# Parking half of the attention results in DRAM, three conversion buffers in the first pass over the weights, and other planner settings

## The chip, the cores and the metric

The kernel runs on one core of a Trainium2 chip. A core has a matrix engine (TensorE, PE in the profile), a vector engine (VectorE, DVE), a scalar engine (ScalarE, ACT), GpSimd (POOL, which here only issues DMAs) and a sync engine (SyncE, SP, which only issues DMAs). They run side by side, each through its own queue in a fixed order, and wait for one another by semaphores. The metric is the device time of one execution in microseconds (us).

## The reference

An attention over 4 batches and 12 heads (448 tokens, 64 columns a head) is followed by one MoE-like block. In short:

```
scores = cap * tanh(q @ k.T / sqrt(64) / cap)
attn   = softmax(scores) @ v                    # per batch and head
x      = heads side by side                     # (4, 448, 768)
u      = x + (x.T @ U @ V).T                    # mixing over the tokens, rank 32
out    = u + max(u @ w_ch1, 0) @ w_ch2          # 768 -> 3072 -> 768
```

`U`, `V`, `w_ch1` and `w_ch2` arrive as 64-bit floats and are read as pairs of 32-bit words. Every product of the block is made of three fp32r matmuls (high by high, high by low, low by high).

## The kernel before, in words

**Attention.** Heads are handled in pairs of 128 rows; a step takes two pairs, so there are 12 steps (three per batch). A step loads q, k and v, makes the scores on PE into PSUM (L417), tanh on ACT with a per-partition scale held in `qsc` (L422), exp on ACT (L430), the products with v on PE (L443, L455), sums of the exponentials on DVE (L462) and a last sum over partitions on PE (L491). The sums go through DMAs from POOL (L496, L501, L514: spread over partitions, to DRAM, back as a broadcast) and scale the result on DVE (L518). Two steps later the mixing follows (`mixin`: transposes L540, high and low parts, products L555 and L576, addition L580). The result of batch b stays in the SBUF tile `u<b>` (128 x 6 x 448).

**Conversion.** The weights are 48 blocks of 128 x 768. Each is loaded as 64-bit words into `wr` (L631, 768 KB), turned into fp32 by four operations (`convert`: an absolute value on ACT L299, a shift L306 on DVE or L304 on ACT, a sign L311 and a join L315 on DVE) and written to DRAM as `kept` (L635). Later it is read back as `wa` (L644). There is one `wr` and one `wc` for most blocks; the first eight may also use a second pair.

**MoE.** Two passes, batches 0 and 1, then 2 and 3; each has 12 chunks of two blocks of w_ch1 and two of w_ch2. In a chunk the up product is done by seven Strassen products of 9 matmuls (L728), whose weight sums `ws` (L601, L608) are made on DVE and ACT from `wa`; the results go through `cx` (L741) and relu (L254, L710) into `g`. The down product has 12 groups of 6 matmuls (L791); three groups stay in PSUM over all chunks (`acc`), the other nine are added to `u` on DVE (L796). A chunk is 135 matmuls. The operands `x` of a pass are made from `u` (L601, L608).

**The order.** A planner in the kernel (`Plan.simulate`) walks through all tasks with a duration for each, a latency for each DMA, a priority and a first time (`begin`), gives every engine its list of instructions, and `emit` writes them out in that order. The numbers in it only set the order: on the chip each engine waits at the head of its own list. Pools (`Pool`) hold SBUF and PSUM room; a pool with `after` opens when the pools named there are closed, and closing waits for everything in them.

**Names that the change touches:** the pools `up` (the four `u` tiles, for the whole kernel), `cv` (one `wr`, one `wc`), `ax` (small attention tiles) and `le`; the constants `ALONE`, `EARLY`, `START`, `PACE`, `NEAR`; the tasks in `convert`, `two`, `normalize`, `mixin`, `converted`, `moe` and `down`.

Of the kernel before, what the change touches and what calls it, by code (L numbers as in the profile page):

```python
# [11 lines left out]
F32 = mybir.dt.float32  # L12
# [3 lines left out]
AF = mybir.ActivationFunctionType  # L16
ALU = mybir.AluOpType
# [15 lines left out]

ALONE = 22

EARLY = 14

# [3 lines left out]

FLOOR = 1

FIRST = 8

START, PACE = 9000, 7000

NEAR = 2

# [223 lines left out]
class Build(Plan):  # L273
    def __init__(self, tc, qk, v, u, vv, w1, w2, cap, ident, out):
        super().__init__()
        self.tc, self.nc = tc, tc.nc
        self.qk, self.v, self.u, self.vv = qk, v, u, vv
        self.w, self.cap, self.id_dram, self.out = (w1, w2), cap, ident, out
        PSUM = bass.MemoryType.PSUM
        self.cp = Pool("cp", {"const": 1})  # L280
        self.up = Pool("up", {"u%d" % b: 1 for b in range(B)})
        self.cv = Pool("cv", {"wr": 1, "wc": 1})
        self.pre = Pool("pre", {"th": 4, "qk": 1, "es": 2, "wr": 1, "wc": 1})
        self.ax = Pool("ax", {"sr": 1, "r7": 2, "rb": 2, "xh": 1, "xl": 1, "ys": 1}, side="right")
        self.ap = Pool("ap", {"qk": 3, "vn": 2, "th": 3, "es": 2}, side="right")
        self.xp = Pool("xp", {"x": 7, "cx": 4, "ta": 2, "wa": 2, "ws": 2}, after=(self.pre,))
        self.lt = Pool("lt", {"ws": 5, "w1": 2, "g": 5}, after=(self.ap,))
        self.le = Pool("le", {"w1": 1, "g": 2}, after=(self.ax,), side="right")
        self.px = Pool("px", {"sc": 1, "o": 1}, space=PSUM, side="right")
        self.ps = Pool("ps", {"sc": 1, "o": 1, "misc": 2}, space=PSUM)  # L290
        self.pm = Pool("pm", {"mm": 3}, after=(self.px,), space=PSUM, side="right")
        self.pl = Pool("pl", {"mm": 5 - len(STAY), "acc": len(STAY)}, after=(self.ps,), space=PSUM)
        self.dp = None

    def convert(self, raw, raw_t, a, a_t, prio, n):
# [5 lines left out]
        def low(e):  # L301
            half = raw_t().bitcast(U16)
            if e is nc.scalar:
                e.activation(out=half[:, 0::4], in_=half[:, 1::4], func=AF.Copy, scale=2.0 ** -13, bias=2.0 ** -14 - 0.5)  # L304
            else:
                e.tensor_scalar(  # L306
                    out=half[:, 0::4], in0=half[:, 1::4], scalar1=13, scalar2=None, op0=ALU.logical_shift_right)
# [11 lines left out]
        self.task({"ACT": 190 + 0.8 * n}, absolute, r=[(raw, "u")], w=[(a, 0)], prio=prio)  # L319
        self.task({"DVE": 1.08 * n, "ACT": 190 + 0.8 * n} if FLOOR else {"DVE": 1.08 * n}, low, r=[(raw, "l")], w=[(raw, "l0")], prio=prio)  # L320
        self.task({"DVE": 1.08 * n}, sign, r=[(raw, "u"), (raw, "l0")], w=[(raw, "l1")], prio=prio)
# [17 lines left out]
    def mixing_consts(self):  # L339
        nc = self.nc  # L340
        begin, prio = 4000, -150
        raw = self.buf("wr", [128, 2 * DM], I32, self.cv, self.pre)
# [23 lines left out]

        self.task({"SP": 700}, load, w=[(raw, "u"), (raw, "l"), ("ident", 0)], lat=4000, begin=begin, prio=prio)
        self.task({"SP": 1400}, load2, w=[(raw2, "u"), (raw2, "l")], lat=4500, begin=begin, prio=prio)
        self.convert(raw, lambda: raw.t[:TM, :2 * n], a, lambda: a.t[:TM, :n], prio, n)
# [4 lines left out]
    def attention(self):  # L374
        self.u_bufs = [self.buf("u%d" % b, [128, NP, S], F32, self.up) for b in range(B)]
        for p in range(0, B * NP + 2 * LAG, 2):
            if p < B * NP:
                self.two(p)
                self.normalize(p + 1)
            if p >= 2 * LAG:  # L380
                self.mixin((p - 2 * LAG) // NP, (p - 2 * LAG) % NP // 2)
# [8 lines left out]
    def two(self, p):  # L390
# [5 lines left out]
        for i, qk in enumerate(qks):  # L396

            def load(i=i, qk=qk):
                nc.sync.dma_start(out=qk.t, in_=self.qk[b, p % NP + i])

            self.task({"SP": 350}, load, w=[(qk, 0)], lat=4000, prio=prio)
        self.task({"SP": 350}, lambda: nc.sync.dma_start(out=vn.t, in_=self.v[b, p % NP // 2]), w=[(vn, 0)], lat=4500, prio=prio)
        REST = (0, 1), 3
        groups = [((0, 0), (0, 1)), ((0, 2), REST), ((1, 0), (1, 1)), ((1, 2),)]
        where = {}
        for steps in groups:
            th = self.buf("th", [128, 2, 2, S], F32, *pools)
            for j, (i, t) in enumerate(steps):
# [12 lines left out]
                def tanh(j=j, ps=ps, th=th):  # L421
                    nc.scalar.activation(out=th.t[:, j], in_=ps.t[:, :, :S], func=AF.Tanh, scale=self.qsc)  # L422

# [55 lines left out]
    def normalize(self, p):  # L479
# [24 lines left out]
        self.task({"DVE": 540, "ACT": 440}, lambda e: self.copy(e, sr.t, s.t[:, :S]), r=[(s, 0)], w=[(sr, 0)], prio=prio)  # L504
        self.task({"POOL": 4000}, spread, r=[(sr, 0)], w=[(r7, 0)], lat=2000, prio=prio)
        self.task({"DVE": 150}, lambda: nc.vector.reciprocal(r7.t, r7.t), w=[(r7, 0)], prio=prio)
        self.task({"POOL": 1000}, put, r=[(r7, 0)], w=[("rd", p)], lat=2500, prio=prio)
        for i, q in enumerate((p - 1, p)):
# [10 lines left out]

            self.task({"POOL": 2000}, get, r=[("rd", p)], w=[(rb, 0)], lat=2900, prio=prio)  # L520
            self.task({"DVE": 538}, norm, r=[(rb, 0)], w=[(u, q % NP)], prio=prio)

    def mixin(self, b, pp):
# [48 lines left out]
        for i in range(2):  # L572
# [9 lines left out]
            self.task({"PE": 210}, mix, r=[(ys, 0), ("vst", 0)], w=[(hh, 0)], prio=prio, mode="mm")  # L582
            self.task({"DVE": 538}, add, r=[(hh, 0)], w=[ks[i]], prio=prio)

    def operands(self, bs, prio):
# [13 lines left out]
    def parts(self, ps, sums, ts, made, terms, n, prio, tag, d, halves):  # L599
# [17 lines left out]
        for p in ps:  # L617
# [3 lines left out]
                w=[(ts[p], 2 * d + 1)], prio=prio)  # L621

    def converted(self, which, f, prio):
        nc = self.nc
        pools = (self.cv, self.pre) if len(self.raws) < FIRST else (self.cv,)
        raw = self.buf("wr", [128, 2 * DM], I32, *pools)
# [9 lines left out]

        self.task({"SP": 350}, load, w=[(raw, "u"), (raw, "l")], lat=4800, prio=prio, begin=START + PACE * (len(self.raws) - 1))
        self.convert(raw, lambda: raw.t, a, lambda: a.t, prio, DM)
        self.task({"ACT": 120}, keep, r=[(a, 0)], w=[("kept", which, f)], lat=5000, prio=prio)

    def block(self, which, f, prio):
        nc = self.nc
        a = self.buf("wa", [128, DM], F32, self.xp)
        self.task({"SP": 350}, lambda: nc.sync.dma_start(out=a.t, in_=self.kept[which, f]),  # L644
            r=[("kept", which, f)], w=[(a, 0)], lat=3500, prio=prio)
        return a
# [29 lines left out]
    def moe(self):  # L676
# [6 lines left out]
        for n, bs in enumerate(((0, 1), (2, 3))):  # L683
            xs = self.operands(bs, -50)
            for c in range(NCH):
                fs = [c * CF + i for i in range(CF)]
                ws = self.strassen_weights(c, 3)
                w1 = {f: self.weights(f, 3) for f in fs}
                gs = {}
# [12 lines left out]
        for _ in self.down(order, *pend):  # L702
            pass

    def relu(self, b, f, src, key, gs):
# [68 lines left out]
    def down(self, order, bs, fs, w1, g, c):  # L774
        nc = self.nc
        last = c == NCH - 1
        for i, b in enumerate(bs):
            u = self.u_bufs[b]
            for d in range(ND):
# [15 lines left out]
                def add(ps=ps, d=d, u=u):  # L795
# [3 lines left out]
                    w=[(ps, 0)], prio=at, mode="mm")  # L799
                if last or not stay:  # L800
                    self.task({"DVE": 538}, add, r=[(ps, 0)], w=[(u, d)], prio=-200)
# [62 lines left out]
```

## Time and profile before

| | |
|---|---|
| median of the timed runs | 939.3 us |
| the profiled execution | 933.91 us, of it the span 932.1 us |
| PE busy | 875.0 us, 94% of the span |
| DVE busy | 710.7 us, 76% |
| ACT busy | 443.7 us, 48% |
| DMA | 123.47 MB, 132 GB/s over the span |
| mean granted clock of PE | 0.987 of full speed |

Busy times are averages over stages with different limits, so the stages have to be read apart: attention until about 228 us (its last sum over partitions), the rest of its normalization and mixing until about 262 us with the first MoE chunk beside it, the first pass until about 598 us, and the second pass until 928 us.

### The profile page before, as it was taken

To read this page: it belongs to the slowest core of one execution; us is meant where nothing else is said; L and a number is where in the kernel's file an instruction comes from. 1 tells how busy PE (TensorE), PEld (TensorE's weight loads), DVE (VectorE), ACT (ScalarE), POOL (GpSimd) and SP (SyncE) were. 2 spreads that over 40 slices of the span, in tenths; PEclk is the share of its full clock that TensorE was granted. 3 is DMA by queue.
4 is the path that set the end of the run, shared out by engine and by line. 5 is a ranking of instruction groups with operands and counts; after the bars stand their busy time and mean duration, and the time that the engine had idled before them with its cause. 6 is when DMAs were issued, how large, how long until landed. Compare 5 with 4: busy or idle time off the path is not lost. (4 is left out here: it accounts for less than half of the span.)

```text
span 932.1 us, 11540 instructions
## 1 busy us (share of the span) xinstructions
PE 875.0 (94%) x4320; PEld 686.9 (74%) x4320; DVE 710.7 (76%) x1153; ACT 443.7 (48%) x623; POOL 59.3 (6%) x112
## 2 busy tenths in 40 slices
PE   6879999889598999999999999899999999999998
PEld 2223333335497898888888898799999999999997
DVE  4778989998778788797887979976556666655654
ACT  6988899987434333343334433432222233322320
POOL 0222322232100000000000000000000000000000
PEclk9999999999799999999999999999999999999999
DMA  7675565324644555645555442431121222112113
GB/s 246 223 240 198 168 214 173 107 64 148 200 156 150 169 189 162 210 140 182 187 165 208 139 153 82 150 87 50 36 69 51 69 68 69 36 49 69 51 52 119
DMA packets 41176, 123.47 MB, mean 132 GB/s; under 512 B 6960, under 2 KB 11040, under 8 KB 41120
## 3 DMA queue, kind: packets, MB, share of 16 engines
q1 hardware_dynamic: 29984, 98.17, 33.8%
q10 hardware_dynamic: 6912, 18.88, 5.1%
q0 software_dynamic: 4224, 5.68, 2.1%
q8 instruction: 34, 0.56, 0.2%
q14 instruction: 22, 0.18, 0.1%
HBM read 98.16 MB, written 24.47 MB: 132 GB/s over the span
## 5 line engine op out<-in xcount | busy, mean ns | idle before, releaser
L728 PE MATMUL mm<-x,ws 128*128 128x448 f32 x1512 | 334.7, 369 | 10.3 <-DVE ws L608 5.4
L728 PEld LDWEIGHTS mm<-x,ws 128*128 128x128 f32 x1512 | 284.1, 189 | 40.2 <-DVE cx L741 7.9
L791 PE MATMUL mm<-g,w 128*128 128x448 f32 x1296 | 288.7, 367 | 7.2 <-DVE cx L741 6.7
L791 PEld LDWEIGHTS mm<-g,w 128*128 128x128 f32 x1296 | 242.2, 188 | 31.2 <-DVE cx L741 9.3
L796 DVE TENSOR_TENSOR u<-u,mm 128x448 f32<-128x448 f32 x216 | 132.5, 621 | 85.2 <-PE mm L791 84.3
L791 PE MATMUL acc<-g,w 128*128 128x448 f32 x432 | 99.2, 365 | 0.0
L254 ACT ACTIVATE g<-cx 128x448 fp32r<-128x448 f32 x72 | 41.7, 580 | 119.1 <-DVE cx L741 118.9
L417 PE MATMUL sc<-qk 64*128 64x448 f32 (+1 forms) x384 | 82.9, 596 | 15.7 <-ACT th L422 10.7
L422 ACT ACTIVATE th<-sc,qsc 128x896 f32<-128x896 f32 x84 | 82.2, 1022 | 8.7 <-PE sc L417 6.7
L791 PEld LDWEIGHTS acc<-g,w 128*128 128x128 f32 x432 | 81.0, 188 | 6.8
L254 ACT ACTIVATE cx<-mm 128x448 f32<-128x448 f32 x72 | 39.1, 543 | 97.7 <-PE mm L728 97.5
L254 ACT ACTIVATE ws<-ta 128x384 fp32r<-128x384 f32 x83 | 43.5, 524 | 76.3 <-DVE ta L601 73.3
L430 ACT ACTIVATE th<-th,capt 128x1792 f32<-128x1792 f32 (+1 forms) x48 | 77.5, 1620 | 0.6 <-ACT th L422 0.3
L299 ACT ACTIVATE wc<-wr 128x768 f32<-128x768 f32 (+2 forms) x50 | 45.3, 906 | 60.5 <-DMA kept<-wc 44.6
L417 PEld LDWEIGHTS sc<-qk 64*128 64x128 f32 (+1 forms) x384 | 26.8, 178 | 57.5 <-ACT th L422 32.7
L306 DVE TENSOR_SCALAR wr<-wr 128x768 uint16<-128x768 uint16 (+2 forms) x39 | 40.0, 1026 | 35.9 <-DMA wr<-in_w 27.1
L741 DVE TENSOR_TENSOR cx<-cx,mm 128x448 f32<-128x448 f32 x72 | 44.8, 623 | 28.3 <-PE mm L728 28.0
L455 PE MATMUL o<-th,vn 128*64 128x448 f32 x276 | 58.2, 556 | 0.5 <-ACT th L430 0.4
L608 DVE TENSOR_TENSOR ws<-ta,ws 128x384 fp32r<-128x384 f32 x96 | 53.6, 560 | 4.8 <-ACT ws L254 3.9
L311 DVE TENSOR_SCALAR wr<-wr 128x768 uint16<-128x768 uint16 (+2 forms) x50 | 50.9, 1018 | 5.7 <-ACT wr L304 5.5
L462 DVE TENSOR_TENSOR es<-es,th 128x896 f32<-128x896 f32 (+1 forms) x48 | 51.9, 1080 | 3.8 <-ACT th L430 3.2
L315 DVE SCALAR_TENSOR_TENSOR wc<-wc,wr 128x768 int32<-128x768 int32 (+2 forms) x50 | 47.0, 940 | 2.6 <-ACT wc L299 1.3
(70 smaller groups left out, 692.9 us busy)
## 6 DMA issues: line engine op xcount, KB each, us to landing
wr<-in_w SPq DMA_DIRECT2D x48, 768.0 KB, 5.6
wa<-kept SPq DMA_DIRECT2D x96, 384.0 KB, 3.1
kept<-wc ACTq DMA_DIRECT2D x48, 384.0 KB, 5.8
qk<-in_qk SPq DMA_DIRECT2D x24, 448.0 KB, 4.3
vn<-in_v SPq DMA_DIRECT2D x12, 448.0 KB, 4.4
rb<-rd POOLq DMA_DIRECT2D x48, 112.0 KB, 3.7
out_t<-u SPq DMA_DIRECT2D x24, 224.0 KB, 1.9
r<-sr POOLq DMA_DIRECT2D x48, 1.8 KB, 3.6
```

The costliest lines, as they stand in the source:

```text
L254: e.activation(out=out, in_=in_, func=func)
L311: nc.vector.tensor_scalar(out=half[:, 1::4], in0=half[:, 3::4], scalar1=0x8000, scalar2=None, op0=ALU.bitwise_and)
L315: nc.vector.scalar_tensor_tensor(out=a_t().bitcast(I32), in0=a_t().bitcast(I32), scalar=3, in1=raw_t()[:, 0::2], op0=ALU.logical_shift_lef ...
L417: nc.tensor.matmul(ps.t[out, a, :S], qks[c].t[hd, 1, 128 * t:min(S, 128 * t + 128)], qks[c].t[hd, 0], start=True, stop=True)
L422: nc.scalar.activation(out=th.t[:, j], in_=ps.t[:, :, :S], func=AF.Tanh, scale=self.qsc)
L430: nc.scalar.activation(out=th.t[:, :n], in_=th.t[:, :n], func=AF.Exp, scale=self.capt)
L455: nc.tensor.matmul(o.t[64 * a:64 * a + 64, :S], vn.t[:, 3 * i + t, a], th.t[:, j, a], start=False, stop=t == 2)
L462: e.tensor_tensor(out=out(), in0=in0(), in1=in1(), op=ALU.add)
L608: e.tensor_tensor(out=lo, in0=src(), in1=hi.bitcast(F32), op=ALU.subtract)
L728: nc.tensor.matmul(ps.t[:, :S], ws[p].t[:, wi, sl], xs[p].t[:, xi, d], start=first and n == 0, stop=n == 8, skip_group_check=True)
L791: nc.tensor.matmul(ps.t[:, :S], w1[f].t[:, wi, sl], g[b, f].t[:, gi], start=fresh and f == fs[0] and i == 0, stop=done and f == fs[-1] and ...
L796: nc.vector.tensor_tensor(out=u.t[:, d], in0=u.t[:, d], in1=ps.t[:, :S], op=ALU.add)
```

## The change

The tiles `u2` and `u3` move from the permanent pool into `ax`, which closes after the attention. When a pair of batch 2 or 3 has been mixed, it is written to DRAM (`park`); the room of `ax` becomes the pool `cz` with two more `wr`, two more `wc` and two `st` tiles for the blocks from number 14 on. Before the second pass `cz` closes and the 12 pieces are read back into new tiles `v2` and `v3` (`unpark`). In chunks 1 to 8 of the first pass three of the nine additions to `u` leave DVE: ACT copies the PSUM result into `st` and a DMA from POOL adds it to `u` (`pour`). The scale of tanh is applied to q on DVE. The shift on ACT writes 32-bit words. The planner gets other latencies, priorities and first times (ten blocks from 14 us on every 8 us, the others from 200 us on every 7.7 us).

```diff
-ALONE = 22
-EARLY = 14
+ALONE = 24
+EARLY = 12
...
-START, PACE = 9000, 7000
-NEAR = 2
+LATER = 14
+START, PACE, AHEAD = 14000, 8000, 10
+THEN, STEP = 200000, 7700
+POUR = 3, 7, 11
+POURS = range(1, 9)
+NEAR = 0
...
-        self.up = Pool("up", {"u%d" % b: 1 for b in range(B)})
+        self.up = Pool("up", {"u0": 1, "u1": 1})
...
-        self.ax = Pool("ax", {"sr": 1, "r7": 2, "rb": 2, "xh": 1, "xl": 1, "ys": 1}, side="right")
+        self.ax = Pool("ax", {"u2": 1, "u3": 1, "sr": 1, "r7": 2, "rb": 2, "xh": 1, "xl": 1, "ys": 1}, side="right")
...
-        self.le = Pool("le", {"w1": 1, "g": 2}, after=(self.ax,), side="right")
+        self.le = Pool("le", {"w1": 1, "g": 2}, after=(self.ax,))
+        self.cz = Pool("cz", {"wr": 2, "wc": 2, "st": 2}, after=(self.ax,), side="right")
+        self.ub = Pool("ub", {"v2": 1, "v3": 1}, after=(self.cz,), side="right")
...
-                e.activation(out=half[:, 0::4], in_=half[:, 1::4], func=AF.Copy, scale=2.0 ** -13, bias=2.0 ** -14 - 0.5)
+                e.activation(out=raw_t()[:, 0::2], in_=half[:, 1::4], func=AF.Copy, scale=2.0 ** -13, bias=2.0 ** -14 - 0.5)
...
-            self.task({"SP": 350}, load, w=[(qk, 0)], lat=4000, prio=prio)
+            self.task({"SP": 350}, load, w=[(qk, 0)], lat=6000 if p else 4000, prio=prio)
+            def scale(qk=qk):
+                x = qk.t[:, 0]
+                nc.vector.tensor_scalar(out=x, in0=x, scalar1=self.qsc, scalar2=None, op0=ALU.mult)
+
+            self.task({"DVE": 363}, scale, w=[(qk, 0)], prio=prio)
...
-                    nc.scalar.activation(out=th.t[:, j], in_=ps.t[:, :, :S], func=AF.Tanh, scale=self.qsc)
+                    nc.scalar.activation(out=th.t[:, j], in_=ps.t[:, :, :S], func=AF.Tanh)
...
+            if b >= 2:
+                q = 2 * pp + i
+
+                def park(q=q):
+                    d = self.parked[b, q] = self.dp.tile([128, S], F32, tag="park", name="park", bufs=2 * NP)
+                    nc.sync.dma_start(out=d, in_=u.t[:, q])
+
+                self.task({"SP": 350}, park, r=[ks[i]], w=[("park", b, q)], lat=4000, prio=prio)
...
-        pools = (self.cv, self.pre) if len(self.raws) < FIRST else (self.cv,)
+        pools = (self.cv, self.pre) if len(self.raws) < FIRST else (self.cv, self.cz) if len(self.raws) >= LATER else (self.cv,)
...
-        self.task({"SP": 350}, load, w=[(raw, "u"), (raw, "l")], lat=4800, prio=prio, begin=START + PACE * (len(self.raws) - 1))
+        self.task({"SP": 350}, load, w=[(raw, "u"), (raw, "l")], lat=6600, prio=prio, begin=self.pace(len(self.raws) - 1))
...
         for n, bs in enumerate(((0, 1), (2, 3))):
-            xs = self.operands(bs, -50)
+            if n:
+                self.unpark()
+            xs = self.operands(bs, 3 + n * (NCH - 0.5) / 100 if n else -50)
...
+    def unpark(self):
+        for b in (2, 3):
+            u = self.u_bufs[b] = self.buf("v%d" % b, [128, NP, S], F32, self.ub)
+            for q in range(NP):
+                self.task({"SP": 350}, lambda b=b, q=q, u=u: self.nc.sync.dma_start(out=u.t[:, q], in_=self.parked[b, q]),
+                    r=[("park", b, q)], w=[(u, q)], lat=5000, prio=-50)
...
-                if last or not stay:
+                if bs[0] == 0 and k in POUR and c in POURS:
+                    t = self.buf("st", [128, S], F32, self.cz)
+
+                    def pour(t=t, d=d, u=u):
+                        nc.gpsimd.dma_start(out=u.t[:, d], in_=t.t, accum_op=ALU.add)
+
+                    self.task({"ACT": 440}, lambda t=t, ps=ps: self.copy(nc.scalar, t.t, ps.t[:, :S]), r=[(ps, 0)], w=[(t, 0)],
+                        prio=-200)
+                    self.task({"POOL": 1100}, pour, r=[(t, 0)], w=[(u, d)], lat=4500, prio=-200)
+                elif last or not stay:
                     self.task({"DVE": 538}, add, r=[(ps, 0)], w=[(u, d)], prio=-200)
```

How this moves the instructions is shown at three places. First PE's queue at the end of the attention: the rows from the last step's scores to the first rows of the last mixings. L417 and L432 are scores, L443 to L470 products with v, L491 and L506 the last sum over partitions, L540 to L591 the mixing, L728 and L764 the Strassen products. Before:

```order
L576 MATMUL misc<-vst,ys 128x448 x2
L728 MATMUL mm<-x,ws 128x448 x9
L417 MATMUL sc<-qk 128x448 x2
L443 MATMUL o<-th,vn 64x448 x2
L443 MATMUL misc<-th,vn 64x448 x2
L455 MATMUL o<-th,vn 64x448 x6
L455 MATMUL misc<-th,vn 64x448 x4
L417 MATMUL sc<-qk 128x448 x2
L728 MATMUL mm<-x,ws 128x448 x18
L455 MATMUL misc<-th,vn 64x448 x2
L728 MATMUL mm<-x,ws 128x448 x9
L491 MATMUL misc<-es,ones 32x448 x4
```

and with the change:

```order
L470 MATMUL o<-th,vn 64x448 x6
L591 MATMUL misc<-vst,ys 128x448 x2
L470 MATMUL o<-th,vn 64x448 x6
L764 MATMUL mm<-x,ws 128x448 x9
L506 MATMUL misc<-es,ones 32x448 x4
L555 MATMUL misc<-ident,u_1004 112x128 x4
L570 MATMUL misc<-xh,ust 128x256 x2
L764 MATMUL mm<-x,ws 128x448 x9
L570 MATMUL misc<-xl,ust 128x256 x2
L555 MATMUL misc<-ident,u_1443 112x128 x4
L764 MATMUL mm<-x,ws 128x448 x9
L570 MATMUL misc<-xh,ust 128x256 x2
```

Four Strassen products stood ahead of the last sum, now one does; eight instead of five stand between it and the end of the mixing.

Second, DVE's queue in the middle of the first pass (L306, L311, L315 and L315, L320, L324 are the shift, sign and join of a conversion; `cx` and `u` are the additions that PE waits for). Before:

```order
L667 TENSOR_TENSOR w_3435<-wa,w_3435 128x768
L796 TENSOR_TENSOR u_550<-u_550,mm 128x448 x2
L306 TENSOR_SCALAR wr<-wr 128x768
L741 TENSOR_TENSOR cx<-cx,mm 128x448
L311 TENSOR_SCALAR wr<-wr 128x768
L796 TENSOR_TENSOR u_550<-u_550,mm 128x448
L710 SCALAR_TENSOR_TENSOR g<-cx,g 128x448
L315 SCALAR_TENSOR_TENSOR wc<-wc,wr 128x768
```

and with the change:

```order
L693 TENSOR_TENSOR w_3278<-wa,w_3278 128x768
L315 TENSOR_SCALAR wr<-wr 128x768
L320 TENSOR_SCALAR wr<-wr 128x768
L777 TENSOR_TENSOR cx<-cx,mm 128x448
L832 TENSOR_TENSOR u_560<-u_560,mm 128x448
L324 SCALAR_TENSOR_TENSOR wc<-wc,wr 128x768
L746 SCALAR_TENSOR_TENSOR g<-cx,g 128x448
L777 TENSOR_TENSOR cx<-cx,mm 128x448
```

The steps of a conversion still stand ahead of additions to `cx`, in both. Over chunks 3 to 11 DVE has 349 instructions where it had 348: 90 of conversions instead of 78, and 24 additions to `u` fewer, with 13 more copies and differences of weights.

Third, SP's queue at the end of the first pass (L631 and L657 load raw blocks, L644 and L670 read back converted ones). Before:

```order
L631 DMA wr<-in_w 128x1536
L644 DMA wa<-kept 128x768
L631 DMA wr<-in_w 128x1536
L644 DMA wa<-kept 128x768 x5
L803 DMA out_t<-u_204 128x448 x6
```

and with the change:

```order
L657 DMA wr<-in_w 128x1536 x2
L670 DMA wa<-kept 128x768 x3
L738 DMA v_4638<-park 128x448 x6
L738 DMA v_4661<-park 128x448 x6
L670 DMA wa<-kept 128x768 x5
L848 DMA out_t<-u_182 128x448 x6
```

Two raw loads stand next to each other, and the 12 reads of the parked pieces come between the last raw load and the results of the first pass.

## Rows read from the trace of the kernel before

**Rows 1.** The page: busy time, share of the span, instructions.
```profile
span 932.1 us, 11540 instructions
PE 875.0 (94%) x4320; PEld 686.9 (74%) x4320; DVE 710.7 (76%) x1153; ACT 443.7 (48%) x623; POOL 59.3 (6%) x112
```

**Rows 2.** Windows: stretch, length; busy us of PE, PEld, DVE, ACT, POOL; clock, DMA, GB/s.
```profile
7.00:228.00 221.00, 199.61 (x1050) 76.28 (x1046) 190.28 (x273) 198.79 (x214) 54.52 (x99) 0.98 0.55 177
228.00:237.00 9.00, 8.55 (x51) 6.86 (x50) 7.38 (x13) 4.84 (x10) 1.97 (x4) 1.00 0.66 219
237.00:254.00 17.00, 7.86 (x26) 4.61 (x25) 13.80 (x21) 7.22 (x12) 2.63 (x5) 0.67 0.59 155
...
246.00:250.00 4.00, 2.06 (x7) 1.12 (x5) 2.74 (x3) 1.80 (x3) 0.00 (x0) 0.50 1.04 297
...
262.50:300.00 37.50, 34.79 (x168) 30.94 (x168) 28.66 (x48) 13.64 (x21) 0.00 (x0) 1.00 0.53 170
300.00:550.00 250.00, 240.66 (x1160) 215.63 (x1159) 205.79 (x329) 98.91 (x160) 0.00 (x0) 1.00 0.54 177
550.00:598.40 48.40, 43.04 (x211) 38.90 (x209) 45.51 (x85) 19.40 (x35) 0.00 (x0) 0.99 0.34 116
598.40:928.40 330.00, 329.91 (x1618) 304.70 (x1618) 210.05 (x373) 94.67 (x166) 0.00 (x0) 1.00 0.21 63
```

**Rows 3.** Timeline of PE around 240 us: start, us, engine, instruction, idle before.
```profile
226.17 2.12 PE L728 MATMUL mm<-x,ws 128*128 128x448 f32 x9
228.22 0.96 PE L491 MATMUL misc<-es,ones 128*32 128x448 f32 x8
...
240.62 0.68 PE L576 MATMUL misc<-vst,ys 128*128 128x448 f32 x2 [2.98 <-DVE ys L567]
...
254.28 3.06 PE L728 MATMUL mm<-x,ws 128*128 128x448 f32 x9
```

**Rows 4.** Groups by line and shape on ACT: busy us, mean ns, idle before.
```profile
L422 ACT ACTIVATE th<-sc,qsc 128x896 f32<-128x896 f32 x84 | 82.2, 1022 | 8.7 <-PE sc L417 6.7 <-PE o L455 2.0
L430 ACT ACTIVATE th<-th,capt 128x1792 f32<-128x1792 f32 x36 | 65.0, 1806 | 0.6 <-ACT th L422 0.3
L299 ACT ACTIVATE wc<-wr 128x768 f32<-128x768 f32 x48 | 44.4, 924 | 59.2 <-DMA kept<-wc 44.6 <-DMA wr<-in_w 14.6
...
L304 ACT ACTIVATE wr<-wr 128x768 uint16<-128x768 uint16 x11 | 21.3, 1939 | 14.4 <-DMA wr<-in_w 14.4
...
L430 ACT ACTIVATE th<-th,capt 128x896 f32<-128x896 f32 x12 | 12.7, 1060 | 0.1
...
L254 ACT ACTIVATE u<-o 128x448 f32<-128x448 f32 x17 | 9.4, 554 | 6.5 <-PE o L455 6.5
```

**Rows 5.** What PE's weight loads waited for until 240 us: us, times, longest.
```profile
PEld sc L417 <- ACT th L422: 32.7, 40, 3.7
```

**Rows 6.** Groups by line and shape on DVE.
```profile
L796 DVE TENSOR_TENSOR u<-u,mm 128x448 f32<-128x448 f32 x216 | 132.5, 621 | 85.2 <-PE mm L791 84.3
...
L315 DVE SCALAR_TENSOR_TENSOR wc<-wc,wr 128x768 int32<-128x768 int32 x48 | 46.1, 961 | 2.5 <-ACT wc L299 1.3
...
L256 DVE CAST x<-u 128x448 fp32r<-128x448 f32 x4 | 1.5, 388 | 0.0
```

**Rows 7.** Timeline of DVE in the first pass, 400 to 426 us.
```profile
399.59 0.96 DVE L315 SCALAR_TENSOR_TENSOR wc<-wc,wr 128x768 int32<-128x768 int32 x1
...
405.98 1.06 DVE L306 TENSOR_SCALAR wr<-wr 128x768 uint16<-128x768 uint16 x1 [1.30 <-DMA wr<-in_w]
...
425.67 1.06 DVE L306 TENSOR_SCALAR wr<-wr 128x768 uint16<-128x768 uint16 x1 [2.17 <-DMA wr<-in_w]
```

**Rows 8.** Timeline of PE in the same stretch.
```profile
412.82 1.49 PE L791 MATMUL mm<-g,w 128*128 128x448 f32 x6 [1.26 <-DVE cx L741]
```

**Rows 9.** DMA issues of the page: count, KB each, median us to landing.
```profile
rb<-rd POOLq DMA_DIRECT2D x48, 112.0 KB, 3.7
out_t<-u SPq DMA_DIRECT2D x24, 224.0 KB, 1.9
```

## What the change will do to the time: the prediction on record

> **What bounds the kernel now.** I read the page's totals first: PE is busy 875.0 of 932.1 us [rows 1], so at most some 57 us can be had unless matmuls themselves get shorter, which the change does not touch. The windows by stage show where those 57 us lie [rows 2]. From 598.4 us to 928.4 us PE has no gap: 1618 matmuls in 330.0 us, 204 ns each, so a chunk of 135 costs 27.5 us. This second pass is at its floor and stays as it is. The losses are earlier.
>
> In the attention (7 to 228 us) three engines are nearly full at once: PE 199.6, ACT 198.8, DVE 190.3 of 221 us [rows 2]. ACT is what is waited for: PE's weight loads for the scores stood 32.7 us behind tanh, which empties their PSUM room [rows 5].
>
> From 237 to 254 us PE is busy only 7.9 of 17 us, part of that at a granted clock of 0.50, which is 1.2 of 2.4 GHz [rows 2]. The idle comes from the last normalization and mixing, whose steps wait in DVE's queue (2.98 us before one mixing product); when the Strassen products resume, nine take 3.06 us where they took 2.12 us [rows 3].
>
> In the first pass (262.5 to 598.4 us) the three windows hold 168, 1160 and 211 PE instructions [rows 2]; at 204 ns they need 34.3, 236.6 and 43.0 us, so 3.2, 13.4 and 5.4 us are lost, 22 us in all. The timelines say why. A join of a conversion ends at 400.55 us; only then is the single raw buffer free, and the shift of the next block starts at 405.98 us, its data just landed [rows 7]. Two blocks later the shift starts at 425.67 us: 19.7 us for two, 9.8 us each. Three are in a chunk, 29.5 us, and a chunk takes 250/1160 x 135 = 29.1 us: **the conversion's chain of load and four operations sets the pace of the first pass.** DVE waits at its head for the load, the additions to `cx` stand behind it, and PE waits 1.26 us for one of them [rows 7, 8].
>
> **The change part by part.** The sum is made against the profiled execution, 933.9 us; the median of the runs is 5.4 us above it, and I carry that difference along.
>
> *Attention.* By the order, ACT loses up to the last exp 4 of 14 absolute values (0.92 us), 2 of 5 shifts (1.94 us) and, net, 10 copies like those of 448 columns (0.55 us): 3.7 + 3.9 + 5.5 = 13.1 us [rows 4]. Tanh loses its scale operand; no tanh without it is in the trace. Exp gives 0.833 ns a column ((1806 - 1060)/896), so tanh has 276 ns beyond its columns, a copy from the same PSUM without a scale 181 ns, and the absolute value, whose scale is a plain number, 284 ns [rows 4]. By the copy 95 ns are saved, by the absolute value none. I take the copy, which reads the same memory with the same stride: 84 x 95 ns = 8 us, bounds 0 and 8. The Trainium skill (ScalarE: Activation LUTs, What ACT_TABLE_LOAD costs) gives each per-partition operand 93 ns, which by that page would be 7.8 us here; it gives plain numbers 186 ns in all, and the absolute value's 284 ns do not agree with that.
>
> DVE gains 24 scalings of q, between a cast of that size (0.39 us) and an addition (0.62 us): 9 to 15 us. It loses ten conversion steps (0.96 us) and nine small ones (0.62 us), 15 us [rows 6]. So DVE stays at about 190 us or drops by 6. PE has three Strassen products (27 x 0.204 = 5.5 us) fewer ahead of the last sum. ACT falls to some 178 us, PE with 194 us becomes the fullest. At the 90% it reaches now (199.6/221) it would need 215 us and put the last sum at 222 us; since its most named wait is for the engine that is relieved, I take 218 us, bounds 207 (no gap to speak of, 194/0.97) and 228 (nothing gained, DVE sets it).
>
> *End of the attention.* From the last sum [rows 3] to the end of the mixing it took 34.5 us (228 to 262.5 us) and held five Strassen products and 12 matmuls of the down product, 57 in all. Now eight products and 6 matmuls stand there, 78 or 15.9 us, beside three mixings of some 3 us (in 228 to 237 us PE was busy 8.55 us, three products are 5.5 of them, one mixing nearly the rest [rows 2]): 25 us of PE work to cover the same chain of DMAs and DVE steps. Between 25 us and 34.5 + 21 x 0.204 = 39 us I take 31, so the end falls at 249 us with 6 matmuls (1.2 us) fewer done: **12 us gained**; with the bounds above, from 6 lost (228 + 39 + 1.2) to 29 gained (207 + 25 + 1.2). Parks wait in SP's queue for the additions of the mixing, with q, k and raw loads behind them; the last such loads have a whole step of some 18 us (221/12) of room, so I price that at nothing; without room each would cost its landing, a few us.
>
> *First pass.* With three raw and three `wc` buffers a load can start two blocks ahead, and its landing leaves the chain. DVE then counts by its sum: 205.8 us per 250 us is 24.0 us a chunk now. Over nine chunks it gets 12 conversion steps (0.96 us) and 13 small ones (at most 0.62 us) more and 24 additions (0.62 us) fewer [rows 6]: +4.7 us, half a us a chunk. 24.5 of 27.5 us is 89%, in a fixed order in which some wait will remain. I leave 8 of the 22 us lost: **14 us gained**, bounds 22 (no loss) and -6 (DVE at its present 82%, 29.8 us a chunk).
>
> *Side costs.* The 24 copies into `st` (0.55 us) fall on an ACT that is busy 98.9 of 250 us. The adding DMA is in no trace: nearest are POOL's broadcast loads, 3.7 us for half the bytes, and a store of one such tile, 1.9 us [rows 9]. I take 5 us; at three a chunk and two buffers a copy waits only from 18 us (2 x 27.5/3) on, so the price is nothing between 2 and 18 us. The 12 reads of the parked pieces start only when `cz` has closed. Sixteen DVE instructions, some 10 us, lie between the last join and the first use; at 224 KB each and the 170 GB/s of this pass they need 16 us, but their uses are spread over 70 instructions. Price 0, at worst 6 us. The shifts on ACT (1.94 us) write other words; between half and the same, off the path.
>
> *Sum:* 933.9 - 12 - 14 = 908 us for a profiled execution, **913 us** with the 5.4 us.
>
> **The rivals.**
> 1. *The first pass keeps its pace* (20%). DVE is fuller, and raw loads of blocks 10 to 13 still have one buffer. A conversion step late at the head of DVE's queue then holds `cx` as it does now. For it: the steps still stand ahead of `cx` in the order, and 89% is much. Against: the load's landing, which ended the waits, is gone from the chain. 913 + 14 = 927 us.
> 2. *The attention does not get shorter* (13%): DVE, as full as before and now also ahead of the scores with its scaling, becomes what is waited for. 913 + 12 = 925 us; with the first rival as well 939.
> 3. *Both gains are near their bounds* (6%): 20 and 18 us, 901 us.
> 4. *Slower* (6%): the adding DMA takes longer than two buffers cover. The place is ACT's copy into `st`; ACT then stands with relu behind it, and PE stops. It decides from 18 us of landing on; each us beyond costs 12 us over 24 of them, so 24 us would give 913 + 70 = 983 us. Against it: POOL's landings of 3.7 us [rows 9].
>
> **How the numbers follow.** My forecast has 55%: 913 us, for itself 904 to 922 us. About 2% is what a measurement of this kernel tells from no change, 920.5 and 958 us. Of the forecast a tenth lies above 920.5 us, and of the first two rivals a sixth below it: faster 0.50 + 0.06 + 0.05 = 0.61, slower 0.06, the rest 0.33. The range goes from 899 us (between the forecast's lower end and the third rival) to 932 us, which takes in the first two rivals alone; outside stay the slow case, both of these rivals together, and the best ends.
>
> **What would show it.** The last sum over partitions before 222 us and PE busy at least 12 of the 17 us after the end of the attention at a full clock; ACT's tanh near 930 ns; no DVE wait for `wr` loads to speak of between 300 and 500 us, and a chunk near 28 us; additions by DMA landing within 10 us; the second pass unchanged at 204 ns a matmul. It is wrong if a chunk still takes 29 us, if the scores wait for the scaling of q, or if PE stands between the passes for the parked pieces.

## The result and the profile after

The changed kernel takes 902.9 us against 939.3 us, a ratio of 0.963 (95% interval 0.954 to 0.971); measured once more, 900.6 against 938.0 us, 0.959 (0.955 to 0.963). The forecast was 913 us with a range of 899 to 932. The profiled execution takes 900.23 us, its span 898.5 us. Two single executions, one of the kernel before (3239 us) and the profiled one of a run below (2975 us, with every matmul some three times as long), are left out of all comparisons.

The page's totals, to be held against [rows 1]:

```profile
span 898.5 us, 11687 instructions
PE 866.5 (96%) x4320; PEld 688.5 (77%) x4320; DVE 706.2 (79%) x1166; ACT 430.4 (48%) x634; POOL 85.4 (10%) x136
```

The windows by stage, columns as in [rows 2]: attention, the rest of the mixing, first pass, the change of passes, second pass.

```profile
7.00:206.20 199.20, 190.53 (x1029) 71.07 (x1029) 183.21 (x276) 176.81 (x196) 55.39 (x99) 1.00 0.54 175
206.20:241.50 35.30, 27.75 (x142) 23.52 (x142) 32.96 (x60) 17.97 (x34) 5.10 (x9) 0.90 0.57 184
...
250.00:525.00 275.00, 273.38 (x1329) 248.39 (x1328) 239.39 (x378) 122.60 (x205) 24.69 (x24) 1.00 0.74 234
...
556.00:562.00 6.00, 2.93 (x15) 2.38 (x13) 6.00 (x12) 1.74 (x3) 0.00 (x0) 0.94 0.47 172
562.00:570.00 8.00, 7.24 (x24) 6.50 (x25) 5.73 (x13) 3.52 (x7) 0.00 (x0) 0.62 0.30 90
...
600.00:894.80 294.80, 294.63 (x1454) 272.76 (x1452) 182.74 (x328) 81.80 (x146) 0.00 (x0) 1.00 0.19 61
```

In the attention PE is busy 190.5 of 199.2 us, 96%, where it was 90% [rows 2]. The timeline of PE gives the marks that [rows 3] give for before:

```profile
206.15 0.96 PE L506 MATMUL misc<-es,ones 128*32 128x448 f32 x8
...
234.31 3.30 PE L764 MATMUL mm<-x,ws 128*128 128x448 f32 x9
...
240.98 0.56 PE L591 MATMUL misc<-vst,ys 128*128 128x448 f32 x2
...
562.76 13.37 PE L764 MATMUL mm<-x,ws 128*128 128x448 f32 x52 [3.83 <-DVE ws L631]
```

The last sum over partitions comes at 206.15 us instead of 228.22 us, 22 us earlier. The rest of the mixing takes 35 us as before and again has a stretch at half clock (0.50 from 230 to 237 us; nine products in 3.30 us at 234 us). At 241.5 us PE has as much done as before at 262.5 us: 1029 + 142 PE instructions against 1050 [rows 2] and 117 in 228 to 262.5 us. **The attention with its mixing gave 21 us.** PE's last matmul ends 33.7 us earlier, at 894.6 us instead of 928.3, so **the first pass, with the change of passes, gave 12.7 us.** In the first pass 1329 matmuls in 275 us are 27.9 us a chunk of 135, against 29.1 [rows 2]; at 204 ns they need 271.1 us, so 3.9 us are lost where 13.4 were. The change of passes still loses 6: 39 matmuls, 8.0 us, in the 14 us from 556 to 570. DVE is busy all of the first six. The second pass is what it was (1454 matmuls in 294.8 us, 203 ns each).

ACT's groups, to be held against [rows 4], landings as [rows 9] give them, and what DVE waits for most from 250 to 570 us (us in all, times, longest):

```profile
L437 ACT ACTIVATE th<-sc 128x896 f32<-128x896 f32 x84 | 74.0, 919 | 10.9 <-PE sc L432 8.5 <-PE o L470 2.1
...
L261 ACT ACTIVATE st<-mm 128x448 f32<-128x448 f32 x24 | 13.1, 545 | 20.7 <-PE mm L827 17.2 <-ACT wc L308 1.4 <-issue 1.2
L313 ACT ACTIVATE wr<-wr 128x768 int32<-128x768 uint16 x10 | 9.1, 909 | 0.0
```
```profile
kept<-wc ACTq DMA_DIRECT2D x48, 384.0 KB, 3.4
u<-st POOLq DMA_DIRECT2D x24, 224.0 KB, 3.9
park<-u SPq DMA_DIRECT2D x12, 224.0 KB, 2.5
v<-park SPq DMA_DIRECT2D x12, 224.0 KB, 5.4
```
```profile
DVE cx L777 <- PE mm L764: 18.4, 17, 2.3
```

Tanh went from 1022 to 919 ns, the adding DMA lands in 3.9 us (median; the longest of the 24 takes 10.4), and what DVE waits for in the first pass is no longer a raw load [rows 7] but PE's products.

### The profile page after: what moved, and what is told of

It is laid out like the page before. It is cut to its first block, busy times and chain, and to the rows that moved or that the text cites. A ratio compares the mean times of both kernels' runs of the same rounds, so it can differ in the third digit from the quotient of the medians.

```text
span 898.5 us, 11687 instructions
## 1 busy us (share of the span) xinstructions
PE 866.5 (96%) x4320; PEld 688.5 (77%) x4320; DVE 706.2 (79%) x1166; ACT 430.4 (48%) x634; POOL 85.4 (10%) x136
## 5 line engine op out<-in xcount | busy, mean ns | idle before, releaser
L764 PE MATMUL mm<-x,ws 128*128 128x448 f32 x1512 | 337.2, 369 | 6.8 <-DVE ws L631 5.1
L764 PEld LDWEIGHTS mm<-x,ws 128*128 128x128 f32 x1512 | 286.0, 190 | 34.0 <-DVE ws L631 7.2
L832 DVE TENSOR_TENSOR v<-v,mm 128x448 f32<-128x448 f32 x108 | 66.0, 619 | 68.1 <-PE mm L827 67.9
L827 PE MATMUL acc<-g,w 128*128 128x448 f32 x432 | 97.0, 366 | 0.2 <-DVE w L693 0.2
L432 PE MATMUL sc<-qk 64*128 64x448 f32 (+1 forms) x384 | 81.6, 590 | 8.3 <-DVE qk L414 5.6
L437 ACT ACTIVATE th<-sc 128x896 f32<-128x896 f32 x84 | 74.0, 919 | 10.9 <-PE sc L432 8.5
L261 ACT ACTIVATE ws<-ta 128x384 fp32r<-128x384 f32 x79 | 41.2, 525 | 55.1 <-DVE ta L624 54.1
L432 PEld LDWEIGHTS sc<-qk 64*128 64x128 f32 (+1 forms) x384 | 26.7, 177 | 50.1 <-issue 22.6
L832 DVE TENSOR_TENSOR u<-u,mm 128x448 f32<-128x448 f32 x84 | 52.1, 622 | 11.5 <-PE mm L827 10.8
L470 PE MATMUL o<-th,vn 128*64 128x448 f32 x288 | 59.8, 548 | 0.0
L631 DVE TENSOR_TENSOR ws<-ta,ws 128x384 fp32r<-128x384 f32 x96 | 52.4, 557 | 3.1 <-ACT ws L261 1.3
L320 DVE TENSOR_SCALAR wr<-wr 128x768 uint16<-128x768 uint16 (+2 forms) x50 | 51.0, 1020 | 2.4 <-ACT wr L313 2.0
L693 DVE TENSOR_TENSOR w<-wa,w 128x768 fp32r<-128x768 f32 x48 | 45.8, 956 | 4.5 <-ACT w L261 4.4
```

What stands on the lines that cost most here:

```text
L261: e.activation(out=out, in_=in_, func=func)
L320: nc.vector.tensor_scalar(out=half[:, 1::4], in0=half[:, 3::4], scalar1=0x8000, scalar2=None, op0=ALU.bitwise_and)
L432: nc.tensor.matmul(ps.t[out, a, :S], qks[c].t[hd, 1, 128 * t:min(S, 128 * t + 128)], qks[c].t[hd, 0], start=True, stop=True)
L470: nc.tensor.matmul(o.t[64 * a:64 * a + 64, :S], vn.t[:, 3 * i + t, a], th.t[:, j, a], start=False, stop=t == 2)
L631: e.tensor_tensor(out=lo, in0=src(), in1=hi.bitcast(F32), op=ALU.subtract)
L693: e.tensor_tensor(out=w.t[:, 1], in0=a.t, in1=w.t[:, 0].bitcast(F32), op=ALU.subtract)
```

## The experiments

Parts of the change can be undone one by one, or done alone in the kernel before. `EARLY`, `NEAR`, the later start of the mixing's constants and the new priorities were not undone on their own. Each run has its own comparison with the kernel before on the same chip (937.3 to 938.0 us).

**The change once more.**

> The changed kernel once more, beside the next three. Every theory: 897 to 908 us, last sum over partitions near 206 us, end of the mixing near 241 us, no loss on PE from 250 to 525 us.

900.58 us, ratio 0.959 (0.955 to 0.963). The last sum comes at 206.77 us. This is the base for what follows.

**Without the extra raw buffers.**

```diff
-LATER = 14
+LATER = 99
```

> The changed kernel with LATER = 99: all late blocks have one raw and one wc buffer again, the rest is as changed. Theory (the chain of load, four operations and next load set the pace of the first pass): 38 blocks at 9.8 us each from about 213 us end near 585 us, the first pass ends 30 to 40 us later, 930 to 940 us; DVE waits for raw loads again. Rival (the additions by DMA and the longer latencies gave the first pass its gain): at most 910 us.

968.98 us, ratio 1.032 (1.027 to 1.037): not the gain undone, but 68 us lost, and slower than before. Nothing changes in the attention (last sum 206.26 us). The windows of this run show when it goes wrong:

```profile
300.00:350.00 50.00, 49.33 (x239) 44.27 (x238) 38.07 (x63) 20.05 (x34) 5.51 (x6) 1.00 0.66 197
350.00:400.00 50.00, 44.42 (x206) 39.23 (x206) 38.71 (x63) 19.56 (x33) 3.98 (x4) 0.97 0.63 181
...
450.00:500.00 50.00, 38.72 (x162) 32.60 (x161) 33.45 (x51) 15.63 (x24) 3.16 (x4) 0.91 0.64 182
500.00:550.00 50.00, 35.00 (x152) 30.47 (x151) 29.79 (x44) 14.80 (x23) 2.61 (x3) 0.85 0.69 221
```

At first the pass runs at full pace; from 350 us on it starves, and the granted clock falls with it. The waits in SP's queue (250 to 640 us) and PE's (250 to 600 us) name the cause:

```profile
SPq L670 <- DMA kept<-wc: 127.2, 24, 7.8
```
```profile
PE mm L764 <- DVE ws L263: 27.0, 6, 11.4
```

The reload of a converted block (`wa`, L670) stands until that block has just been written: the stock of blocks is used up. Neither before nor the change has such a wait. Counting joins, before has 16 blocks converted by 250 us and makes the other 32 in 9.9 us each ((557.3 - 250.5)/31); this run has 13 and makes 35 in 10.2 us each. A chunk uses four in 27.5 us, 6.9 us each. So a single buffer, at 10 us a block, works only on a stock, and the change enters the pass with a smaller one. With three buffers it makes a block in 7.4 us ((506.7 - 256.4)/34).

**Without pours.**

```diff
-POURS = range(1, 9)
+POURS = range(0)
```

> The changed kernel without additions by DMA: 24 of them go back to DVE (POURS empty). Theory: DVE goes from 23.9 to about 25.5 of 27.5 us a chunk, still below PE's time, so 0 to 4 us slower, 900 to 907 us. Rival (DVE's relief by the additions made the first pass run at PE's pace): a chunk goes back towards 29 us, 912 us or more.

900.99 us, ratio 0.960 (0.956 to 0.963): no difference. DVE then has the 24 additions again and keeps the pace:

```profile
250.00:525.00 275.00, 271.14 (x1321) 247.07 (x1320) 247.68 (x389) 109.69 (x184) 0.00 (x0) 1.00 0.60 213
```

1321 instead of 1329 matmuls. DVE at 90% busy does not hold the first pass, which my first rival supposed.

**The scale back on tanh.**

```diff
-            self.task({"DVE": 363}, scale, w=[(qk, 0)], prio=prio)
...
-                    nc.scalar.activation(out=th.t[:, j], in_=ps.t[:, :, :S], func=AF.Tanh)
+                    nc.scalar.activation(out=th.t[:, j], in_=ps.t[:, :, :S], func=AF.Tanh, scale=self.qsc)
```

> The changed kernel with the scale back on tanh and no scaling of q on DVE. Theory (ACT was what the attention waited for): ACT gets 84 x 0.10 us = 8.7 us more, the last sum moves from 206 to about 211 us, total 4 to 6 us slower. Rival (PE and DVE set the attention's length now, tanh's scale does not matter): last sum within 2 us of 206 us, and since DVE is 9 us freer perhaps earlier.

906.9 us, ratio 0.966 (0.962 to 0.971), last sum 211.41 us: 4.6 us of the 22 (against the run beside it). Tanh takes 1014 ns with the operand.

**The old pace of conversions.**

```diff
-START, PACE, AHEAD = 14000, 8000, 10
+START, PACE, AHEAD = 9000, 7000, 48
```

> The change with one thing undone: weight blocks are converted during the attention at the old pace (first at 9 us, one every 7 us, no pause) instead of ten of them and then a pause until 200 us. Theory (part of the 22 us that the attention won is conversions that no longer stand on ACT and DVE there): the last sum, at 206.2 us with the change, comes at 211 to 217 us, the first pass gets blocks early and keeps its 27.9 us per chunk, and the whole time is 904 to 910 us against 900.6. Rival (the conversions hide in the attention, and all 22 us are tanh without its operand and the planner's other order): last sum at 205 to 208 us, whole time within 3 us of 900.6.

944.04 us, ratio 1.009 (1.006 to 1.012). Theory and rival both fell. The attention loses 2.2 us only (last sum 208.40 us): 12 blocks are made by 228 us against 11 in the change, so it was not the pace that thinned them out there. But from 250 us on blocks come in 4.4 us each, and this is what the first pass looks like:

```profile
300.00:350.00 50.00, 34.66 (x143) 28.96 (x144) 46.88 (x66) 24.68 (x37) 4.96 (x4) 0.86 0.97 334
350.00:400.00 50.00, 40.59 (x175) 35.56 (x174) 45.86 (x66) 24.93 (x39) 2.92 (x3) 0.86 0.89 321
...
450.00:500.00 50.00, 50.00 (x249) 46.38 (x248) 28.61 (x52) 18.13 (x34) 4.34 (x5) 1.00 0.32 78
```

The DMA engines are busy 97%, DVE 94%. The three streams of this run between 290 and 400 us land in:

```profile
wr<-in_w SPq DMA_DIRECT2D x24, 768.0 KB, 6.2
kept<-wc ACTq DMA_DIRECT2D x27, 384.0 KB, 6.4
wa<-kept SPq DMA_DIRECT2D x12, 384.0 KB, 6.9
```

In the same stretch of the change `wa` lands in 3.6 us and `kept` in 3.8 us. PE's longest waits in that stretch, though, are for weights that DVE has to make (products of the up and of the down matmuls):

```profile
PE mm L764 <- DVE ws L631: 13.3, 5, 4.8
...
PE acc L827 <- DVE w L693: 8.4, 3, 5.9
```

DVE waits only 1.8 us there for a reload, ACT 8.7 us. So the weights of the running chunk come late behind blocks for chunks that are far off, in DVE's queue above all; what the slower landings add to that was not separated. Once all blocks are made PE is full again.

**The same dose behind the attention alone.**

```diff
-THEN, STEP = 200000, 7700
+THEN, STEP = 200000, 4000
```

> The change with one number altered: from 200 us on a weight block may start every 4.0 us instead of every 7.7 us. Nothing before 200 us can differ. Theory (three raw buffers are not the whole of the gain in the first pass: blocks must also not come faster than chunks use them, or raw loads and kept stores fill the DMA engines and the weights of the running chunk come late, as they did with the old pace): 11 to 13 blocks per 50 us between 250 and 400 us, DMA share above 0.85 and PE below 45 of 50 us there, whole time 925 to 950 us against 900.6. Rival (the old pace lost its time through what it did to the attention and the order behind it): first pass at 27.9 us per chunk, whole time within 5 us of 900.6.

930.25 us, ratio 0.991 (0.988 to 0.995): the time that the theory gave, 30 us lost by the pace alone. The attention is untouched: the order of the instructions on PE, DVE and ACT is that of the change until some 255 us of its trace. The block rate, the DMA share and PE's share that the theory names are not shown by this run. Buffers and pace belong together: too few blocks starve the chunk, too many crowd it out.

**Only the planned DMA times, in the kernel before** (three of the nine lines).

```diff
-            self.task({"SP": 350}, load, w=[(qk, 0)], lat=4000, prio=prio)
+            self.task({"SP": 350}, load, w=[(qk, 0)], lat=6000 if p else 4000, prio=prio)
...
-            self.task({"POOL": 2000}, get, r=[("rd", p)], w=[(rb, 0)], lat=2900, prio=prio)
+            self.task({"POOL": 2000}, get, r=[("rd", p)], w=[(rb, 0)], lat=4500, prio=prio)
...
-            r=[("kept", which, f)], w=[(a, 0)], lat=3500, prio=prio)
+            r=[("kept", which, f)], w=[(a, 0)], lat=5500, prio=prio)
```

> The kernel before with one thing of the change: the planner's DMA times (raw blocks 6.6 us, kept 6.3, weights back 5.5, q and k 6.0, v 6.5, spread 3.0, row 4.5); no parking, no second raw buffer, no pours. Theory (the first pass was held by the one raw buffer, which true times in the plan do not widen): chunk of the first pass 28.8 us or more, whole time 930 to 942 us against 938; a better order in the attention may give up to 5 us. Rival (the first pass was held by an order planned with times that were too short): chunk at most 28.2 us and whole time 918 to 926 us.

967.64 us, ratio 1.033 (1.029 to 1.037). Both fell, and in an instructive way: the last sum comes 8.8 us earlier (219.45 us), and the first pass then starves as it does without extra buffers. SP's reload waits for blocks just written (250 to 640 us):

```profile
SPq L644 <- DMA kept<-wc: 113.5, 20, 11.2
```

By 250 us 15 blocks are made instead of 16, then one every 10.9 us, where before made one every 9.9 us.

**Only tanh without its operand, in the kernel before.**

```diff
+            def scale(qk=qk):
+                x = qk.t[:, 0]
+                nc.vector.tensor_scalar(out=x, in0=x, scalar1=self.qsc, scalar2=None, op0=ALU.mult)
...
-                    nc.scalar.activation(out=th.t[:, j], in_=ps.t[:, :, :S], func=AF.Tanh, scale=self.qsc)
+                    nc.scalar.activation(out=th.t[:, j], in_=ps.t[:, :, :S], func=AF.Tanh)
```

> The kernel before with q scaled on DVE and the tanh without its scale operand, and nothing else of the change. Theory (ACT sets the attention's pace before, 102 ns a tanh in 84 tanh is worth the 5 us that putting it back into the change cost): last sum at 222 to 225 us instead of 228.2, whole time 931 to 935 us against 938. Rival (with conversions at the old pace DVE is as full, and takes back what ACT gives): last sum after 226.5 us, whole time 936 us or more.

970.42 us, ratio 1.034 (1.028 to 1.040). The last sum comes at 225.67 us, 2.6 us earlier, between the two expectations, and the pass starves again: 14 blocks by 250 us, one every 10.4 us, and

```profile
SPq L649 <- DMA kept<-wc: 61.7, 11, 10.8
```

In both runs a faster attention stands in a slower kernel. How much of the 30 us in these two runs is the missing stock and how much the fixed order, in which conversion steps queue behind work that is already late, is not separated.

**The old planned times, in the change** (two of the nine lines).

```diff
-            self.task({"POOL": 2000}, get, r=[("rd", p)], w=[(rb, 0)], lat=4500, prio=prio)
+            self.task({"POOL": 2000}, get, r=[("rd", p)], w=[(rb, 0)], lat=2900, prio=prio)
...
-            r=[("kept", which, f)], w=[(a, 0)], lat=5500, prio=prio)
+            r=[("kept", which, f)], w=[(a, 0)], lat=3500, prio=prio)
```

> The change with the planner's DMA times put back to those of before (raw blocks 4.8 us, kept 5.0, weights back 3.5, q and k 4.0, v 4.5, spread 2.0, row 2.9). Theory (the planned times won in the attention what they won alone in the kernel before, where the last sum came 8.8 us earlier, and tanh without operand the other part): last sum at 211 to 217 us instead of 206.2, whole time 906 to 918 us. Rival (in this kernel ACT's relief alone gives the shorter attention): last sum at 205 to 208 us, whole time within 4 us of 900.6.

916.77 us, ratio 0.976 (0.971 to 0.981); the last sum comes at 219.35 us, 13.2 us later: of the parts undone here this is the largest in the attention's gain. The timelines of DVE and PE show one such place:

```profile
59.50 0.68 DVE L566 TENSOR_TENSOR xl<-misc,xh 112x512 fp32r<-112x512 f32 x1
64.11 0.62 DVE L533 TENSOR_TENSOR u<-u,rb 128x448 f32<-128x448 f32 x1 [3.94 <-DMA rb<-rd]
...
66.53 0.68 DVE L566 TENSOR_TENSOR xl<-misc,xh 112x512 fp32r<-112x512 f32 x1
```
```profile
67.27 0.61 PE L570 MATMUL misc<-xl,ust 112*128 112x256 f32 x2 [3.95 <-DVE xl L566]
```

The normalization's multiplication is ordered as if its row landed in 2.9 us. It stands 3.94 us at DVE's head; `xl` is queued behind it, and PE waits 3.95 us for `xl` at the head of its own queue. A second place like it costs PE 2.1 us at 101 us. In before the same multiplication stood 5.3 us in three places; in the change, with the longer times, it stands 2.7 us in two. Most of the nine new times lie above the landing (a row 4.5 us planned, 3.1 to 3.7 us measured; a reload 5.5 us planned, 3.1 us measured). Which of them matter, and whether it is the match or the slack that helps, was not tried.

**Two heads with one PSUM tile each.**

```diff
-ALONE = 24
+ALONE = 22
```

> The change with ALONE = 22 as before: the last two heads' scores and outputs use only one PSUM tile each instead of two, and the MoE's three banks open that much earlier. Theory (a smaller part of the 22 us comes from these tiles): last sum at 208 to 212 us instead of 206.2, some of it repaid by Strassen products done earlier, whole time 901 to 908 us. Rival (no part of it): last sum at 205.5 to 207.5 us, whole time 898 to 902 us.

912.72 us, ratio 0.972 (0.966 to 0.978), last sum 213.90 us: 7.7 us later, more than the theory allowed, and nothing of it is repaid behind. The single steps (4.6, 2.2, 13.2 and 7.7 us) come to more than 22 us: they overlap.

**Sums of the second pass on POOL too.**

```diff
+POOLD = 1100
...
-                self.task({"DVE": dve(n)}, partial(term, p=p, a=a, op=op, b=b), r=[*ka, *kb],
-                    w=[(sums[p], 0)], prio=prio)
+                on = {"DVE": dve(n), "POOL": POOLD} if tag == "cx" and prio > 0 else {"DVE": dve(n)}
+                self.task(on, partial(term, p=p, a=a, op=op, b=b), r=[*ka, *kb], w=[(sums[p], 0)], prio=prio)
```

> The change, with the twelve sums of the second pass's operands allowed on POOL as well as on DVE (planned at 1.1 us there). Theory (between 556 and 570 us the PE waits for DVE, which is busy all of the time): up to twelve times 0.53 us leave DVE, the stall of 3.8 us before the second pass shrinks to 0 to 2 us and the stretch at the lower clock behind it goes, whole time 895 to 899 us against 900.6. Rival (POOL's sums are slower than planned, or slow DVE down while they run): DVE operations in that stretch longer by 0.2 us or more, whole time 900 us or more.

904.12 us, ratio 0.965 (0.962 to 0.969): no gain, the rival. POOL took seven sums. Its timeline and that of DVE beside it:

```profile
546.89 1.16 POOL L626 TENSOR_TENSOR cx<-cx,v 128x448 f32<-128x448 f32 x1 [0.56 <-DVE x L633]
548.12 1.18 POOL L626 TENSOR_TENSOR cx<-v,cx 128x448 f32<-128x448 f32 x1
```
```profile
546.73 0.61 DVE L834 TENSOR_TENSOR u<-u,mm 128x448 f32<-128x448 f32 x1
547.26 1.03 DVE L265 CAST x<-v 128x448 fp32r<-128x448 f32 x1
548.21 1.57 DVE L633 TENSOR_TENSOR x<-cx,x 128x448 fp32r<-128x448 f32 x1
549.71 0.61 DVE L834 TENSOR_TENSOR u<-u,acc 128x448 f32<-128x448 f32 x1
```

While POOL sums, a subtraction of two SBUF tiles takes 1.57 us instead of 0.61 and a cast 1.03 instead of 0.38; an addition with one input from PSUM (546.73 us), most of it beside POOL's sum, keeps its 0.61. DVE loses what it hands over. The Trainium skill (GPSIMD Engine Reference, Key points) says that GpSimd shares its SBUF interfaces with VectorE and contends with its instructions that have two SBUF inputs or run in a 2-port performance mode. The trace agrees for the subtraction; whether the cast runs in such a mode no row shows.

**Blocks resumed later, no pours.**

```diff
-THEN, STEP = 200000, 7700
+THEN, STEP = 225000, 7000
-POURS = range(1, 9)
+POURS = ()
```

> The change without any pour, and with the blocks after the tenth allowed from 225 us on, one every 7.0 us, instead of from 200 us, one every 7.7 us. Theory (behind the last sum the mixing's steps and the first Strassen weights wait in DVE's queue, and two conversions of 3 us stand among them; without them the mixing ends 3 to 6 us earlier; the pours were worth nothing): mixing's last product at 235 to 238 us instead of 241, whole time 894 to 899 us. Rival (the tail is held by the normalization's DMAs, not by DVE; blocks come too late for the third chunk): last product at 240 us or later, whole time 900 us or more.

894.72 us, ratio 0.953 (0.950 to 0.956): the best of all, some 6 us under the change's 900.6 us, whose interval (0.955 to 0.963) it just touches. Leaving out the pours alone changed nothing, so the later pace is the likelier cause. The mechanism expected did not happen: the mixing's last product comes at 242.26 us, no earlier. What changed is how much PE does beside the mixing:

```profile
206.20:241.50 35.30, 31.39 (x166) 27.22 (x165) 31.26 (x60) 16.32 (x33) 4.59 (x9) 0.95 0.42 135
...
250.00:525.00 275.00, 273.73 (x1337) 249.47 (x1336) 258.98 (x413) 116.93 (x192) 0.00 (x0) 1.00 0.64 223
```

In the stretch of the mixing lie 166 PE instructions instead of 142, 24 x 0.204 = 4.9 us: 12 more of Strassen products and 14 more of the down product, and two of the mixing not yet done. Only 11 blocks are made by 250 us, but the others in 6.8 us each, and no reload waits more than 1.1 us. DVE is at 94% in the first pass and PE at 99.5%.

## Why the prediction was right, and where not

The time lies in the stated range, but under the 904 to 922 us that the forecast gave itself, and it is in the range because the range reached down towards the third rival. For a profiled execution the sum said 908 us and 900.2 were measured: the attention gave 9 us more than forecast, the first pass 1.3 us less. The 5.4 us that I added from the profiled execution to the median were 2.7 us for the changed kernel, which is no merit of the sum.

**Attention: right in sign, mis-sized.** I put the last sum at 218 us, bound 207; it came at 206.15. The term that failed is "At the 90% it reaches now ... I take 218 us". ACT's relief and PE's work came out as counted (176.8 us on ACT for 178, 190.5 on PE for 194), and so did tanh: 103 ns saved, from 1022 to 919 ns, where I had 95. The Trainium skill (ScalarE: Activation LUTs, What ACT_TABLE_LOAD costs) gives such an operand 93 ns; the 103 ns, and the 95 ns when it was put back (1014 ns), are near that. But the relief of tanh was only 2.6 to 4.6 us of the 22, by the two runs on it. I took PE's occupancy as a property of the kernel; it was a property of the order. The longer DMA times in the plan give 8.8 us alone in before and 13.2 us in the change, and the PSUM tiles at the end up to 7.7 us. I had counted the rows that moved and not asked what the longer `lat` values move, although `rb`'s 3.7 us against a planned 2.9 us stood in [rows 9].

**End of the attention: not shorter.** 31 us forecast, 35 us measured, with 25 more PE instructions where I counted 21. PE is busy 14.5 of the 17 us behind 206.2 us at full clock, the sign that I had asked for, but most of its waits and the half clock come later. It waits 5.6 us for mixing steps of DVE and 1.9 us for those of ACT, and DVE is busy 33 of the 35.3 us; I had looked at PE's work and the DMA chain. That DVE's fullness holds the end of the mixing is not shown: with conversions taken out of that stretch the end came no earlier. With the last sum this made 21 us instead of 12.

**First pass: the size right, the reason half.** 14 us forecast, 12.7 us measured. The load did leave the chain, DVE's waits for it are gone, and DVE is at 87% where I counted 89%; even at 94%, in the last run, it left PE busy 99.5%. Yet "the conversion's chain sets the pace" was too small a picture: a chunk uses four blocks where the chain made three, so it drains a stock. Without the extra buffers the change would not have missed 14 us but lost 68: it enters the pass earlier and with 13 blocks instead of 16. The gains of attention and buffers are not two terms of a sum: in these runs the first paid only with the second.

**Side costs: as priced.** Pours land in 3.9 us for 5 (the longest, 10.4 us, is past the 10 us that I had set, without harm) and are worth nothing either way; the fourth rival did not come. The shift on ACT took half. The change of passes, "price 0, at worst 6 us", still loses 6 us, about what it lost before (5.4 [rows 2]): not for the parked pieces, which no engine but SP waits for (1.2 us); PE waits for weight sums that stand on DVE behind operands and additions, and the granted clock is then 0.62 for 8 us.

The third rival, both gains near their bounds (901 us, 6%), came closest in time, but by its attention alone: 21 us for its 20. The first pass gave 12.7 us for its 18, as my own forecast had it.

## What to carry to other kernels

Where a planner writes the order, its latencies decide what stands at an engine's head: compare each planned latency with the landing in the trace before counting busy time; a plan that expects a landing too early puts a waiting instruction at the head. A stream that is made ahead of use has a rate and a stock; check that rate x time + stock covers the use before shortening what comes before, and pace it at the rate of use, since faster crowds out the work that is due. Undoing one part of a bundle shows what that part is worth to the others, not what it is worth alone.

## What the hardware showed

- ACT's shift of 768 values writes 16-bit words at a stride in 1939 ns [rows 4], and 32-bit words in 909 ns.
- The store of a converted block lands in 5.7 or 5.8 us (median) with one raw buffer, with and without the rest of the change, and in 3.4 us in the change with three, but in 5.0 us in the last run, which has three too. That the raw load, which the same join releases, shares the engines with it might explain part of this; it was not tried.
- A sum of 128 x 448 on POOL takes 1.15 to 1.52 us and can more than double a DVE subtraction beside it (1.57 us for 0.61).
